# Two more ring buffers, gate exponentials in pieces, six early tiles of the heads' product, and mixed zero products

## The chip, the cores and the metric

The kernel runs on one core of a Trainium2 chip. The metric is device time in microseconds (us), the median of several runs. A profile of one further execution is used for reading; its times are those of that execution.

## The reference

The input is x of 2048 tokens by 512 channels. Two branches are computed and mixed by a gate for each token; everything is float32.

```python
qkv = x @ wqkv                       # 32 heads of 16 channels
p = softmax(q @ k.T * 16 ** -0.5)    # full, 2048 x 2048 for each head
a = (p @ v) @ wo
b = (sigmoid(x @ w_gate) * (x @ w_up)) @ w_down      # 1792 hidden channels
g = sigmoid((x * gate_w).sum(-1))
out = g * a + (1 - g) * b
```

## The kernel before

**Precision.** Products that need float32 accuracy are split: each operand into a high part (type fp32r) and a low part (the remainder), and three products of parts are added up in PSUM. "Split" below means making these two parts, usually a copy on one engine and a subtraction on another (`split`, or `split_later` for steps that are queued for POOL).

**Order.** TensorE, ScalarE (ACT), VectorE (DVE) and GpSimd (POOL) run their instructions in the order in which the program issues them. The DMAs are all issued from SyncE's queue (SP), whose order a scheduler chooses. Tiles come from pools; a tile with a `tag` and `bufs=n` takes the place of the one that was given out n allocations earlier, and its first writer waits until the last user of that one is done, a DMA out of it included.

**The start.** A column `warm` of zeros is set, and `WARM = 10` products of zeros (line 83, 128 x 128 by 128 x 512) go to TensorE while x and the first weights come in. Then queries and keys of the first 128 channels are computed (line 585), then the values `v` and the first maxima.

**The main loop.** It has `NPER = 256` steps k. Heads are taken in pairs, 16 steps for a pair. A step computes eight blocks of scores of 128 x 512 (`st_part`, line 619, four for each head, called t0 and t1 in the orders), whose exponentials ACT writes to `p` (line 621), and at its end the products of p and v (`values`, line 755). The result is copied out of PSUM (`part`, line 760 on ACT; on DVE, line 762, once the maxima have ended) and added up on POOL (line 772). In the same steps TensorE computes scores a second time, ten steps ahead, for the row maxima (`sm_step`, line 268, called m0 and m1), which DVE reduces (line 270). The maxima end ten steps before the last.

**The dense sums.** Beside this a generator `filling` gives out dense products in small sums: queries and keys of the other heads (`qk`), then gate and up products in a scheme with fewer multiplications (`far`, `side`, `chain`), and last `heads`: the product of the attention's result with `wo`, for the first tokens and for the first two of four row blocks. All of these sums use one PSUM bank, `dn`. The matmuls of a sum use half of the PE's rows each (line 152) so that they run beside score matmuls on the other half; d1 are those on the upper half, d0 on the lower. Between the halves `turn` puts a nop on POOL (line 163): it waits for the last matmul of one half, and the first of the other waits for it. So this hand-over stands in POOL's order, behind whatever POOL was given before. `work` hands the queued POOL steps out, after each turn and at the end of each step.

A finished sum is copied out of `dn` by `out_of` (line 429 on DVE, 558 on ACT) into a tile of the ring `er`, which has four buffers, and is then stored to DRAM or added. `put_mix` (lines 332 and 338, tiles `mh` and `ml`) splits mixtures of x during the `far` sums, also into `er`, and stores them to `t_d`.

**The orders.** What TensorE does in a step is written out as a string. `STEADY` has six d1 and six d0 and the maxima; `MORE`, in the three steps after the maxima have ended (k = 246 to 248), has no maxima; `LAST`, in the seven steps after these, has three d1 and three d0. So a sum of twelve half matmuls takes one step in STEADY and MORE and two in LAST. The sums are 252 in all.

**The early hidden chunks.** The hidden layer is processed in 28 chunks. For the first two of them gate and up are loaded at k = 241 (`hidden_load`, into buffers that the queries and keys of a finished pair leave), and `hidden_early` computes the sigmoid in steps: the exponential of the gate on ACT (line 698, 128 x 1024, one call at k = 243 and one at k = 244, issued after the values and their copy), then 16 steps on DVE (lines 702 to 715), one at k = 245 and three in each step from k = 246.

**The tail.** After the loop come 28 chunks of the down projection (line 939), with the hidden layer's sigmoid on ACT (line 691) and its splits, and eight tiles of 256 tokens of the heads' product with `wo` (`heads_out`, line 139). For tiles u < 4, whose first two row blocks were done in the loop and lie in `hp_d`, only the other two are multiplied here, and the stored part is loaded (`had`, one tile of a single buffer) and added (line 922). `finish` applies the gate and stores the output.

Of the kernel before, what the change touches and what calls it, by code (L numbers as in the profile page):

```python
# [25 lines left out]
P = 128  # L26
# [10 lines left out]
WARM = 10  # L37
# [3 lines left out]
BOTH = FREE + 3  # L41
# [5 lines left out]
def gated_mix(ctx, tc, x, xT, wqk, wv, wo, w_gate, w_up, w_down, gate_w, out):  # L47
# [26 lines left out]
    hp_d = dram.tile([8, P, D], F32, name="hp_d")  # L74
# [7 lines left out]
    for _ in range(WARM):  # L82
        pe.matmul(banks[2], z.to_broadcast([P, P]), z.to_broadcast([P, 512]), start=True, stop=True)
# [123 lines left out]
    def put_first(o, dst, c):  # L207

        if c % 2:
            e = [keep.tile([P, 512], F32R, name=f"qe{i}_{c}", tag="er", bufs=4) for i in range(2)]  # L210
        else:
            e = keep.tile([P, 2, 512], F32R, name=f"qe_{c}", tag="ev", bufs=2)
            e = [e[:, i, :] for i in range(2)]
# [115 lines left out]
    def put_mix(n, c, k, t):  # L329
        def high():  # L330
            h = out[n, c, k] = keep.tile([P, 512], F32R, name=f"mh{n}_{c}{k}", tag="er", bufs=4)
# [3 lines left out]
        def low():  # L335
            h = out.pop((n, c, k))
            l = keep.tile([P, 512], F32R, name=f"ml{n}_{c}{k}", tag="er", bufs=4)
# [21 lines left out]
    def filling():  # L359
# [67 lines left out]
        def out_of(run, name):  # L427
            e = keep.tile([P, 512], F32, name=name, tag="er", bufs=4)
# [6 lines left out]
        def sums_of(kind, n, ws):  # L435
# [27 lines left out]
            elif kind == "heads":  # L463
                for u in range(4):
# [49 lines left out]
        def first_heads_split(u):  # L514
            oh, ol, ot, rb = first_heads(u)
            e = keep.tile([P, 2, 256], F32, name=f"of{u}", tag="er", bufs=4)
# [7 lines left out]
        for job, nxt in zip(jobs, jobs[1:]):  # L524
            kind, n = job
            coming = None
            for at, run in enumerate(sums_of(kind, n, ws)):
# [7 lines left out]
                if job == ("chain", pairs[-1]):  # L535
                    if at == 4:
                        for u in range(4):
# [3 lines left out]
                if kind == "heads" and at in (2, 4):  # L541
                    first_heads_split(at // 2 + 1)
# [151 lines left out]
    def hidden_early(m):  # L694
# [3 lines left out]
        act.activation(gate, gate, AF.Exp, scale=-1.0)  # L698
        yield
# [108 lines left out]
    MORE = "t0 d1 t0 d1 d1 t0 d1 d1 t0 d1 turn t1 d0 t1 d0 d0 t1 d0 d0 t1 d0"  # L808
# [6 lines left out]
    for k in range(NPER):  # L815
# [13 lines left out]
        emit(STEADY if k < FREE else MORE if k < BOTH else LAST, **parts)  # L829
# [9 lines left out]
        if k == NPER - 1:  # L839
            break  # L840
        spot[:] = [seven[SUMS]]
        values(k)
        if k == NPER - 15:
            loaded.extend(hidden_load(*chunks[m]) for m in range(2))
            early = [hidden_early(m) for m in range(2)]
        if 192 <= k < 202:
# [5 lines left out]
        if k == NPER - 13:  # L852
            next(early[0])
        if k == NPER - 12:
            next(early[1])
            early = chain(*early)
        if k >= NPER - 11:
# [20 lines left out]
    def heads_load(u):  # L878
        ot = lp.tile([P, KT, 256], F32, name=f"ot{u}", tag="ot")
        rb = lp.tile([P, KT, 256], F32, name=f"rb{u}", tag="rb")  # L880
        ks = slice(2 if u < 4 else 0, KT)
        o_and_r(u, range(KT)[ks], ot[:, ks], rb[:, ks])
        if u < 4:
            had[u] = lp.tile([P, 2, D], F32, name=f"had{u}", tag="had")
            sp.dma_start(had[u], hp_d[2 * u:2 * u + 2].rearrange("a p d -> p a d"))
        return ot[:, ks], rb[:, ks]

    def heads_split(u, ot, rb):
        ks = slice(2 if u < 4 else 0, KT)
# [23 lines left out]
    def heads_out(u, hl):  # L913
        for a in range(2):
            o = bankh()
            cols = slice(a * P, (a + 1) * P)
            ks = range(2 if u < 4 else 0, KT)
# [76 lines left out]
```

## Time and profile before

| | us |
|---|---|
| median of 3 runs | 1703.01 |
| lowest, highest | 1702.22, 1705.33 |
| profiled execution, its own time | 1706.67 |
| span of the profile | 1704.9 |
| ACT, exponentials of scores (line 621), mean of one | 0.63 to 0.65 |
| POOL, additions of values (line 772), mean of one | 1.29 |
| ACT, gate exponentials (line 698), two of them, each | 1.05 |

Times in the profile count from the start of the span. The views used are the page with its engine shares, the waits (who waited for whom), the chain of work that ended last in order of time, the timeline of one engine (start, duration, engine, line, operation, output and inputs, count, and in brackets the idle time before it and what ended it), and the stretches (busy time of each engine between two times, with the clock granted to TensorE and the DMA engines' load). A row of the chain gives the start, the duration, the engine and the line. Half of TensorE's matmuls run beside another one, so a row's duration is not its share of the time; the distance from one start to the next is.

### The profile page before, as it was taken

To read this page: it belongs to the slowest core of one execution; us is meant where nothing else is said; L and a number is where in the kernel's file an instruction comes from. 1 tells how busy PE (TensorE), PEld (TensorE's weight loads), DVE (VectorE), ACT (ScalarE), POOL (GpSimd) and SP (SyncE) were. 2 spreads that over 40 slices of the span, in tenths; PEclk is the share of its full clock that TensorE was granted. 3 is DMA by queue.
4 is the path that set the end of the run, shared out by engine and by line. 5 is a ranking of instruction groups with operands and counts; after the bars stand their busy time and mean duration, and the time that the engine had idled before them with its cause. 6 is when DMAs were issued, how large, how long until landed. Compare 5 with 4: busy or idle time off the path is not lost.

```text
span 1704.9 us, 34507 instructions
## 1 busy us (share of the span) xinstructions
PE 1694.7 (99%) x12498; PEld 1036.1 (61%) x12498; DVE 1446.6 (85%) x2336; ACT 1357.8 (80%) x2638; POOL 883.6 (52%) x865
## 2 busy tenths in 40 slices
PE   9999999999999999999999999999999999999999
PEld 7755555555555555555555555555555555567887
DVE  6988888888789999989888888889988888797643
ACT  4188888888798888988889889889898898884331
POOL 1034343447664555555566666676666666653110
PEclk9999999999999999999999999999999999999999
DMA  9312324254646343433635353535353533458962
GB/s 255 87 40 68 84 63 95 64 126 154 180 151 159 113 106 107 111 116 101 188 104 141 107 143 101 144 107 136 104 126 109 130 113 132 158 186 275 312 199 72
DMA packets 127178, 224.55 MB, mean 132 GB/s; under 512 B 23264, under 2 KB 33248, under 8 KB 124128
## 3 DMA queue, kind: packets, MB, share of 16 engines
q1 hardware_dynamic: 127008, 222.36, 45.4%
q8 instruction: 98, 1.61, 0.4%
q14 instruction: 72, 0.59, 0.1%
HBM read 131.86 MB, written 90.44 MB: 130 GB/s over the span
## 4 chain that ended last, share of the span: by engine, by line
PE 93%; DMA 4%; DVE 2%; SPq 1%; POOL 1%; issue 1%; ACT 0%; DVEq 0%; POOLq 0%; ACTq 0%
PE dn L152 29%; PE sm L755 26%; PE sm L268 12%; PE st L619 7%; PE sm L619 4%; PE sm L939 4%; PE st L268 2%; PE dn L939 2%; PE st L152 1%; PE st L139 1%; DMA gul<-gu_d 1%; PE st L585 1%; PE st L939 1%; PE sm L139 1%; DMA wd0r<-in_w_down_dram 0%
## 5 line engine op out<-in xcount | busy, mean ns | idle before, releaser
L270 DVE TENSOR_REDUCE stat<-sm 128x1 f32<-128x512 f32 x1310 | 848.4, 683 | 161.0 <-PE sm L619 138.7
L621 ACT ACTIVATE p<-st 128x512 f32<-128x512 f32 x1020 | 615.4, 650 | 2.1 <-PE st L619 2.1
L621 ACT ACTIVATE p<-sm 128x512 f32<-128x512 f32 x1026 | 606.4, 626 | 6.1 <-PE st L619 2.8
L268 PE MATMUL sm<-ks,qs 48*128 48x512 f32 x1310 | 522.7, 437 | 0.1
L755 PE MATMUL sm<-p,v 128*17 128x512 f32 x4032 | 483.4, 597 | 0.0
L270 DVE TENSOR_REDUCE stat<-st 128x1 f32<-128x512 f32 x738 | 482.2, 681 | 0.1
L619 PE MATMUL sm<-qs,ks 64*128 64x512 f32 x1026 | 429.5, 421 | 0.7 <-ACT p L621 0.7
L619 PE MATMUL st<-qs,ks 64*128 64x512 f32 x1020 | 427.8, 420 | 0.0
L268 PEld LDWEIGHTS sm<-ks,qs 48*128 48x128 f32 x1310 | 238.5, 184 | 294.1 <-DVE stat L270 208.8
L772 POOL TENSOR_TENSOR sum<-sum,part 128x512 f32<-128x512 f32 x224 | 289.1, 1291 | 184.3 <-PE sm L619 165.6
L268 PE MATMUL st<-ks,qs 48*128 48x512 f32 x738 | 291.6, 395 | 0.0
L760 ACT ACTIVATE part<-sm 128x512 f32<-128x512 f32 x215 | 128.7, 599 | 138.3 <-issue 106.7
L755 PEld LDWEIGHTS sm<-p,v 128*17 128x17 f32 x4032 | 93.5, 97 | 228.1 <-issue 158.7
L619 PEld LDWEIGHTS st<-qs,ks 64*128 64x128 f32 x1020 | 188.0, 184 | 29.4 <-issue 3.4
L619 PEld LDWEIGHTS sm<-qs,ks 64*128 64x128 f32 x1026 | 189.6, 185 | 11.9 <-issue 4.3
L496 POOL TENSOR_TENSOR chain<-chain,chain 128x512 f32<-128x512 f32 x84 | 108.5, 1292 | 114.8 <-PE sm L619 103.7
L268 PEld LDWEIGHTS st<-ks,qs 48*128 48x128 f32 x738 | 137.7, 187 | 1.6 <-ACT p L621 0.4
L496 POOL TENSOR_TENSOR had<-chain,had 128x512 f32<-128x512 f32 x84 | 108.2, 1288 | 55.3 <-PE sm L619 44.3
L496 POOL TENSOR_TENSOR side<-side,side 128x512 f32<-128x512 f32 x28 | 36.2, 1291 | 93.2 <-PE sm L619 89.7
L558 ACT ACTIVATE chain<-dn 128x512 f32<-128x512 f32 x112 | 77.9, 696 | 0.0
L102 POOL TENSOR_TENSOR ol<-ot,oh 128x512 fp32r<-128x512 f32 (+1 forms) x8 | 15.3, 1915 | 99.9 <-ACT oh L99 79.9
L692 DVE TENSOR_TENSOR gul<-gul 128x1024 f32<-128x1024 f32 x26 | 41.7, 1603 | 19.1 <-DMA gul<-gu_d 11.8
(879 smaller groups left out, 3204.9 us busy)
## 6 DMA issues: line engine op xcount, KB each, us to landing
gul<-gu_d SPq DMA_DIRECT2D x56, 512.0 KB
had<-gu_d SPq DMA_DIRECT2D x84, 256.0 KB
gu_d<-had SPq DMA_DIRECT2D x84, 256.0 KB
gu_d<-side SPq DMA_DIRECT2D x56, 256.0 KB
qs<-q_d SPq DMA_DIRECT2D x90, 128.0 KB
ks<-k_d SPq DMA_DIRECT2D x90, 128.0 KB
pv_d<-sum SPq DMA_DIRECT2D x32, 256.0 KB
gu_d<-far SPq DMA_DIRECT2D x28, 256.0 KB
```

Source lines behind the costliest of these rows:

```text
L152: mm = pe.matmul(self.o, a[rows], b[rows], start=(self.n == 0), stop=(self.n == 2 * len(self.ops) - 1))
L268: pe.matmul(t, qs[r:r + KM, qt * P:(qt + 1) * P], ks[r:r + KM, g * 512:(g + 1) * 512], start=True, stop=True)
L270: dve.tensor_reduce(stat[half][:, b, qt % 8, g:g + 1], t, axis=AX.X, op=ALU.max)
L496: pool.tensor_tensor(to, u, w, ALU.add)
L558: leave = lambda e, o: act.activation(e, o, AF.Copy)
L619: pe.matmul(o, ks[r:r + KR, (kt + a) * P:(kt + a + 1) * P], qs[r:r + KR, q0:q0 + 512], start=True, stop=True)
L621: act.activation(pt[:, 2 * a + c, :], o, AF.Exp, scale=DH ** -0.5)
L692: dve.tensor_tensor(gu[:, 1], gu[:, 0], gu[:, 1], ALU.mult)
L755: pe.matmul(o[32 * c:32 * c + VW, :], v[:, 2 * k % 16 + a, h * VW:(h + 1) * VW], pts[c // 2][:, 2 * a + c % 2, :], start=(a == 0), stop=(a ...
L760: act.activation(e, o, AF.Copy)
L772: pool.tensor_tensor(s, s, e, ALU.add)
L939: pe.matmul(down[t], a, b, start=(f == 0 and m == 0), stop=(f == NF - 2 and m == 5))
```

## The change

Four things change.

1. The ring `er` has six buffers, not four, everywhere it is used. In the tail `had` is no tile of its own pool any more: it is two `er` tiles for each u, loaded by two DMAs of 256 KB and not by one of 512 KB.
2. The gate exponentials are issued as four activations of 128 x 256 for each chunk. Two are issued in each of the steps k = 242 to 245, ahead of the values matmuls and so ahead of ACT's copy `part` of that step. The loads move from k = 241 to k = 239. The DVE steps start at k = 243, one a step up to k = 245 and three a step from k = 246.
3. `EARLY = 3`: three tiles of 256 tokens (six sums of 128) are given their first two row blocks in the loop, not four (eight sums). The sums are now 250. `MORE` is gone, and `LAST` is used for all ten steps from k = 246. In the tail u = 3 is multiplied with all four row blocks, and its loads and splits are those of u = 4 to 7.
4. The ten products of zeros are replaced by a mix: twice, four float32 products on the lower 64 rows (one on each strip of 17 columns, 256 wide) and two fp32r products on the upper 64 rows (256 wide); then four of 256 and two of 512 on all rows.

```diff
@@ -34,11 +34,10 @@
 KM = 3 * DH
 KR = 64
 LEAD = 20
-WARM = 10
 NSTEP = NPAIR * 32
 NPER = NSTEP // 2
 FREE = NPER - LEAD // 2
-BOTH = FREE + 3
+EARLY = 3
 HF = NF // 2
 LOW, UP = 0, 1
 
@@ -71,7 +70,7 @@
     k_d = dram.tile([2, D, S], F32, name="k_d")
     gu_d = dram.tile([2, NF, P, S], F32, name="gu_d")
     pv_d = dram.tile([2, NPAIR, P, 512], F32, name="pv_d")
-    hp_d = dram.tile([8, P, D], F32, name="hp_d")
+    hp_d = dram.tile([2 * EARLY, P, D], F32, name="hp_d")
     rec_d = dram.tile([P, 512], F32, name="rec_d")
     t_d = dram.tile([3, 2, 2, 2, P, 512], F32, name="t_d")
     max_d = dram.tile([2 * NPAIR, 4, 32, 2, 32], F32, name="max_d")
@@ -79,8 +78,20 @@
     warm = keep.tile([P, 1], F32, name="warm")
     dve.memset(warm, 0.0)
     z = warm.bitcast(F32R)
-    for _ in range(WARM):
-        pe.matmul(banks[2], z.to_broadcast([P, P]), z.to_broadcast([P, 512]), start=True, stop=True)
+
+    def zeros(o, a, b, r=slice(0, P)):
+        rows, m, n = r.stop - r.start, o.shape[0], o.shape[1]
+        pe.matmul(o, a[r].to_broadcast([rows, m]), b[r].to_broadcast([rows, n]), start=True, stop=True)
+    low, up = slice(0, 64), slice(64, P)
+    for _ in range(2):
+        for c in range(4):
+            zeros(banks[2][32 * c:32 * c + VW, :256], warm, warm, low)
+        for _ in range(2):
+            zeros(banks[1][:, :256], z, z, up)
+    for _ in range(4):
+        zeros(banks[1][:, :256], z, z)
+    for _ in range(2):
+        zeros(banks[2], z, z)
     mpads = [keep.tile([P, 32], F32, name=f"mpad{i}") for i in range(2)]
     mpad = turns(mpads)
     den = keep.tile([P, 512], F32, name="den")
@@ -207,7 +218,7 @@
     def put_first(o, dst, c):
 
         if c % 2:
-            e = [keep.tile([P, 512], F32R, name=f"qe{i}_{c}", tag="er", bufs=4) for i in range(2)]
+            e = [keep.tile([P, 512], F32R, name=f"qe{i}_{c}", tag="er", bufs=6) for i in range(2)]
         else:
             e = keep.tile([P, 2, 512], F32R, name=f"qe_{c}", tag="ev", bufs=2)
             e = [e[:, i, :] for i in range(2)]
@@ -328,13 +339,13 @@
 
     def put_mix(n, c, k, t):
         def high():
-            h = out[n, c, k] = keep.tile([P, 512], F32R, name=f"mh{n}_{c}{k}", tag="er", bufs=4)
+            h = out[n, c, k] = keep.tile([P, 512], F32R, name=f"mh{n}_{c}{k}", tag="er", bufs=6)
             pool.tensor_copy(h, t)
             sp.dma_start(t_d[n, 0, c, k], h.bitcast(F32))
 
         def low():
             h = out.pop((n, c, k))
-            l = keep.tile([P, 512], F32R, name=f"ml{n}_{c}{k}", tag="er", bufs=4)
+            l = keep.tile([P, 512], F32R, name=f"ml{n}_{c}{k}", tag="er", bufs=6)
             pool.tensor_tensor(l, t, h.bitcast(F32), ALU.subtract)
             sp.dma_start(t_d[n, 1, c, k], l.bitcast(F32))
         out = {}
@@ -425,7 +436,7 @@
             return ws[0], ws[2], ws[1], ws[3]
 
         def out_of(run, name):
-            e = keep.tile([P, 512], F32, name=name, tag="er", bufs=4)
+            e = keep.tile([P, 512], F32, name=name, tag="er", bufs=6)
             leave(e, run.o)
             return e
 
@@ -461,7 +472,7 @@
                         else:
                             plus(e, e, first, place(m, i, c + 2))
             elif kind == "heads":
-                for u in range(4):
+                for u in range(EARLY):
                     while split_of[u] in later:
                         later.pop(0)[1]()
                     oh, ol = [t for t in first_heads(u)][:2]
@@ -513,7 +524,7 @@
 
         def first_heads_split(u):
             oh, ol, ot, rb = first_heads(u)
-            e = keep.tile([P, 2, 256], F32, name=f"of{u}", tag="er", bufs=4)
+            e = keep.tile([P, 2, 256], F32, name=f"of{u}", tag="er", bufs=6)
             later.append((1.3, lambda: pool.tensor_tensor(e, ot.bitcast(F32), rb.bitcast(F32), ALU.mult)))
             split_later(oh, ol, e)
             split_of[u] = later[-1]
@@ -534,12 +545,12 @@
                         mix_x(u // 2, u % 2)
                 if job == ("chain", pairs[-1]):
                     if at == 4:
-                        for u in range(4):
+                        for u in range(EARLY):
                             first_heads_load(u)
                     if at in (6, 7):
                         first_heads_split(at - 6)
-                if kind == "heads" and at in (2, 4):
-                    first_heads_split(at // 2 + 1)
+                if kind == "heads" and at == 2:
+                    first_heads_split(2)
                 if at == ask[kind][0]:
                     coming = raws(*nxt)
                 if at == ask[kind][1]:
@@ -695,8 +706,10 @@
 
         gu = loaded[m]
         gate, up = [gu[:, a].rearrange("p f s -> p (f s)") for a in range(2)]
-        act.activation(gate, gate, AF.Exp, scale=-1.0)
-        yield
+        for a in range(4):
+            cols = slice(a * 256, (a + 1) * 256)
+            act.activation(gate[:, cols], gate[:, cols], AF.Exp, scale=-1.0)
+            yield
         two = [slice(a * 512, (a + 1) * 512) for a in range(2)]
         for cols in two:
             dve.tensor_scalar(gate[:, cols], gate[:, cols], 1.0, 3e38, op0=ALU.add, op1=ALU.min)
@@ -805,7 +818,6 @@
     STEADY = ("m1:3 t0:2 m0:4 d1 d1 t0:5 m0:6 d1 d1 t0:1 d1 m0:3 d1 t0:2 turn m0:0 t1:4 "
               "m1:5 d0 d0 t1:1 t1:6 d0 m1:2 d0 m1:3 d0 t1:4 d0")
     SUMS = 0
-    MORE = "t0 d1 t0 d1 d1 t0 d1 d1 t0 d1 turn t1 d0 t1 d0 d0 t1 d0 d0 t1 d0"
     LAST = "t0 d1 t0 d1 t0 d1 turn t0 t1 t1 d0 t1 d0 t1 d0"
 
     parts = {"m0": mx(0), "m1": mx(1), "d0": dense(LOW), "d1": dense(UP)}
@@ -826,7 +838,7 @@
         if n % 32 == 0 and n // 32 + 1 < NPAIR:
             load_pair(n // 32 + 1)
         parts["t0"], parts["t1"] = st_part(k, 0), st_part(k + 1, 1) if k + 1 < NPER else iter(())
-        emit(STEADY if k < FREE else MORE if k < BOTH else LAST, **parts)
+        emit(STEADY if k < FREE else LAST, **parts)
         if run and run.done():
             run = next(fill, None)
         elif run and run.n:
@@ -838,11 +850,15 @@
         soon.clear()
         if k == NPER - 1:
             break
+        if NPER - 15 < k <= NPER - 11:
+            for _ in range(2):
+                next(next(exps))
         spot[:] = [seven[SUMS]]
         values(k)
-        if k == NPER - 15:
+        if k == NPER - 17:
             loaded.extend(hidden_load(*chunks[m]) for m in range(2))
             early = [hidden_early(m) for m in range(2)]
+            exps = iter([early[0]] * 4 + [early[1]] * 4)
         if 192 <= k < 202:
             next(dens[0], None)
         if k == NPER - 6:
@@ -850,11 +866,8 @@
         if k == NPER - 2:
             raws = [late_raw(*late[m][:2]) for m in range(2)]
         if k == NPER - 13:
-            next(early[0])
-        if k == NPER - 12:
-            next(early[1])
             early = chain(*early)
-        if k >= NPER - 11:
+        if k >= NPER - 13:
             for _ in range(1 if k < FREE else 3):
                 next(early, None)
 
@@ -878,15 +891,16 @@
     def heads_load(u):
         ot = lp.tile([P, KT, 256], F32, name=f"ot{u}", tag="ot")
         rb = lp.tile([P, KT, 256], F32, name=f"rb{u}", tag="rb")
-        ks = slice(2 if u < 4 else 0, KT)
+        ks = slice(2 if u < EARLY else 0, KT)
         o_and_r(u, range(KT)[ks], ot[:, ks], rb[:, ks])
-        if u < 4:
-            had[u] = lp.tile([P, 2, D], F32, name=f"had{u}", tag="had")
-            sp.dma_start(had[u], hp_d[2 * u:2 * u + 2].rearrange("a p d -> p a d"))
+        if u < EARLY:
+            had[u] = [keep.tile([P, D], F32, name=f"had{u}_{a}", tag="er", bufs=6) for a in range(2)]
+            for a in range(2):
+                sp.dma_start(had[u][a], hp_d[2 * u + a])
         return ot[:, ks], rb[:, ks]
 
     def heads_split(u, ot, rb):
-        ks = slice(2 if u < 4 else 0, KT)
+        ks = slice(2 if u < EARLY else 0, KT)
         oh = lp.tile([P, KT, 256], F32R, name=f"oh{u}", tag="oh", bufs=2)[:, ks]
         ol = lp.tile([P, KT, 256], F32R, name=f"ol{u}", tag="ol", bufs=2)[:, ks]
         dve.tensor_tensor(ot, ot, rb, ALU.mult)
@@ -914,11 +928,11 @@
         for a in range(2):
             o = bankh()
             cols = slice(a * P, (a + 1) * P)
-            ks = range(2 if u < 4 else 0, KT)
+            ks = range(2 if u < EARLY else 0, KT)
             product(o, [((hl[0][:, n, cols], hl[1][:, n, cols]), (wohl[:, 0, k, :], wohl[:, 1, k, :]))
                         for n, k in enumerate(ks)])
-            if u < 4:
-                h = had[u][:, a]
+            if u < EARLY:
+                h = had[u][a]
                 dve.tensor_tensor(h, o, h, ALU.add)
                 o = h
             finish(2 * u + a, o, g1)
```

## The prediction

> **What bounds the kernel now.** I read the page's engine shares first, then the waits of TensorE, then the chain of work in order of time, then the stretches around each edit. The engine share, from the page:
>
> ```profile
> PE 1694.7 (99%) x12498; PEld 1036.1 (61%) x12498; DVE 1446.6 (85%) x2336; ACT 1357.8 (80%) x2638; POOL 883.6 (52%) x865
> ```
>
> TensorE is never idle to speak of, so an edit pays only where it takes matmuls away, or one of TensorE's few waits, or a stretch in which another engine paces it. The waits of TensorE itself (us in total, times, longest):
>
> ```profile
> PE dn L152 <- POOLq L163: 2.5, 2, 2.1
> PE sm L939 <- DVE hl L102: 1.0, 1, 1.0
> ...
> PE sm L619 <- ACT p L621: 0.7, 2, 0.4
> ```
>
> There are three families: the hand-over nop of a dense sum on POOL (line 163), ScalarE's exponentials, and the tail's splits. What each is worth is read from the chain in order of time. The L755 blocks (16 matmuls of the values) mark the steps k, one block in each:
>
> ```profile
> 381.46 1.84 PE sm L755 x16
> ...
> 395.01 2.16 DMA t_d<-mh
> 399.03 1.84 PE sm L755 x16
> ...
> 443.74 1.89 PE sm L755 x16
> ...
> 454.87 5.71 DMA gu_d<-far
> 464.35 3.54 PE sm L755 x16
> 471.63 1.84 PE sm L755 x16
> 477.21 1.84 PE sm L755 x16
> ...
> 1422.84 1.84 PE sm L755 x16
> ```
>
> An undisturbed step is 477.21 - 471.63 = 5.58 us. From 381.46 to 399.03 are three steps: 17.57, which is 0.83 over 16.74. From 443.74 to 477.21 are five: 33.47, which is 5.57 over 27.90. A DMA out of a buffer of the dense sums' ring stands in the chain both times.
>
> **Part 1, the ring `er` from four to six.** On POOL, ahead of the second stall, and the stretch behind it (columns: us, busy of PE, PEld, DVE, ACT, POOL, then granted clock, DMA share, GB/s):
>
> ```profile
> 455.68 1.27 POOL L338 TENSOR_TENSOR ml<-mix,mh 128x512 fp32r<-128x512 f32 x1
> 460.70 0.61 POOL L332 CAST mh<-mix 128x512 fp32r<-128x512 f32 x1 [3.75 <-DMA gu_d<-far]
> ```
>
> ```profile
> 461.40:464.30 2.90, 2.88 (x15) 1.85 (x16) 1.16 (x2) 1.39 (x3) 2.90 (x3) 0.50 0.50 190
> ```
>
> The cast `mh` takes the slot that a `far` sum left four allocations earlier. That sum's store was issued only at 454.87 and landed 5.71 later. The nop of line 163 stands behind the cast in POOL's order, and TensorE behind the nop. With six slots the cast takes the slot of an allocation two places older, a `far` tile of an earlier step whose store was issued before the jam. The cast would then start at 456.95, when `ml` ends, and the nop would be out at about 457.6; TensorE, which waited 2.1 us until the cast was done at 461.3, came to it at about 459.2. The wait is 2.1 us, yet the excess is 5.57, because the granted clock stands at 0.50 afterwards and a values block takes 3.54 instead of 1.84. [...] The stall at 395.01 is of the same kind (POOL waits for `t_d<-mh`, four allocations back). Both gone: **-6.40**. The bound the other way is 0, if other waits take their place.
>
> **Part 2, the gate exponentials.** Before, two 1024-wide activations stand behind the values copy `part` of steps 243 and 244. After, eight of 256 stand ahead of the copies of steps 242 to 245, two in each. On ScalarE:
>
> ```profile
> 1457.01 0.70 ACT L558 ACTIVATE chain<-dn 128x512 f32<-128x512 f32 x1
> 1458.28 0.60 ACT L760 ACTIVATE part<-sm 128x512 f32<-128x512 f32 x1 [0.58 <-POOL chain L496]
> 1458.78 1.05 ACT L698 ACTIVATE gul<-gul 128x1024 f32<-128x1024 f32 x1
> ```
>
> ```profile
> 1514.22 0.22 ACT L866 ACTIVATE g<-logit 128x16 f32<-128x16 f32 x1
> 1514.34 1.05 ACT L691 ACTIVATE gul<-gul 128x1024 f32<-128x1024 f32 x1
> ```
>
> A 512-wide activation occupies ScalarE for 0.50 us, start to next start (1458.28 to 1458.78), a 16-wide one for 0.12 (1514.22 to 1514.34). In a straight line between them a 256-wide one takes 0.30 and a pair 0.61. The engine is free from 1457.51 (0.50 after the sum's copy began) to 1458.28: 0.77 us, in which `part` waits for the values matmuls. The pair fits. If a piece took all of 0.50, a pair would overrun by 0.23, 0.9 us over four steps. The price of the old place is in the chain rows: from 1422.84 to 1469.31 (next fence) are eight steps, 46.47 against 44.64. That **-1.83** goes; I take no overrun. The old activations were no TensorE stop worth the name (0.4 each), but TensorE was paced by ScalarE until it had caught up.
>
> The gate and up loads move with them, past two steps of SP's queue: four issues of 512 KB, now right behind the early heads' loads, of which a quarter (four) fall away. Queued behind them on SP are loads and stores of `had`, for which POOL's adds and then the line 163 nop wait. VectorE's first three steps of `hidden_early` move into steps 243 to 245, behind the values, where VectorE idles in each step:
>
> ```profile
> 1458.63 0.69 DVE L270 TENSOR_REDUCE stat<-sm 128x1 f32<-128x512 f32 x1 [0.71 <-PE sm L619]
> ```
>
> Two of them are short and lie in that 0.71 us; the third, a reciprocal, comes when the maxima are over. They cost nothing.
>
> **Part 3, six tiles instead of eight, and LAST three steps earlier.** Chain rows, and VectorE's copy of a dense sum:
>
> ```profile
> 1469.31 1.84 PE sm L755 x16
> ...
> 1474.51 1.84 PE sm L755 x16
> ...
> 1484.87 1.84 PE st L755 x16
> ...
> 1488.70 1.84 PE st L755 x16
> ...
> 1492.54 1.84 PE st L755 x16
> ...
> 1496.71 1.84 PE sm L755 x16
> ```
>
> ```profile
> 1493.95 0.68 DVE L429 COPY hp<-dn 128x512 f32<-128x512 f32 x1
> ```
>
> Steps 247 and 248 (MORE) take (1484.87 - 1474.51)/2 = 5.18 each; a LAST step takes 1492.54 - 1488.70 = 3.84. MORE carries a whole dense sum in a step, LAST half of one; with 250 sums, not 252, the remaining four fit into eight LAST steps. Three steps save 3 x 1.34 = 4.02. One LAST step took 4.17: the only bank `dn` was still being copied by VectorE at 1493.95, behind three steps of `hidden_early`. With every sum in LAST steps I add one more such wait: +0.33, net **-3.69**. LAST is eight exponentials a step, so ScalarE paces it.
>
> The missing tiles return in the tail. The heads of u = 3 multiply two row blocks before and four after, as u = 4 already does:
>
> ```profile
> 1605.90 1.36 PE sm L139 x6
> ...
> 1624.94 2.72 PE st L139 x12
> ```
>
> Two tiles of 1.36 become two of 2.72: **+2.72**, all of it on TensorE, which has no gap there. The extra loads, ScalarE and POOL split of u = 3, and the two dropped additions lie beside it. `had` becomes six ring tiles instead of one shared one; that takes waits from SP, or lets those loads run ahead (a rival below).
>
> **Part 4, the mixed zero products.** TensorE, then its weight loads:
>
> ```profile
> 0.92 4.63 PE L83 MATMUL st<-warm 128*128 128x512 f32 x10 [0.92 <-DVE warm L80]
> 5.35 0.63 PE L585 MATMUL st<-xh,q0h 128*128 128x512 f32 x1
> ...
> 7.05 0.50 PE L585 MATMUL st<-xl,q0h 128*128 128x512 f32 x1
> 7.39 0.39 PE L585 MATMUL st<-xh,q0l 128*128 128x512 f32 x1
> ```
>
> ```profile
> 9.24 0.19 PEld L585 LDWEIGHTS st<-xl,q0h 128*128 128x128 f32 x1 [0.29 <-DVE xl L102]
> ```
>
> Ten zeros take (5.35 - 0.92)/10 = 0.44 us each, twice the 0.227 of 2.72/12, up to 7.05. The new ones, at that slow pace: a values block runs two f32 products of 512 columns on each of four strips side by side in 1.84, so one of 256 columns takes 0.46, and 0.92 at half pace; the two fp32r products of half the rows, 0.22 each, run beside it or behind it. Two such rounds are 1.84 to 2.7; then 4 x 0.22 and 2 x 0.44 follow: 3.6 to 4.5 us instead of 4.4. The first product can gain up to 0.35, but at 9.24 the products wait for VectorE's split in any case: **0**.
>
> **Sum.** -6.40 - 1.83 - 3.69 + 2.72 = -9.2 us. The profiled execution took 1706.67 us (span 1704.90, 1.77 around it), so its counterpart comes to 1697.5. It lies 3.66 above the median of 1703.01; I give the unprofiled runs the same difference: **1693.8**.
>
> **The rivals.**
> (a) *The ring's wait is not removed, only moved.* In the same step SP's late issue holds the store, and a sixth slot may be held as well, or POOL's adds may wait for `mix`. For: 3.75 us of POOL waiting is longer than one step's slack. Against: the older slots' stores were issued a step earlier. Then 5.57 stays: 1699.4.
> (b) *The `had` loads run ahead into the tail's opening.*
>
> ```profile
> 1535.00:1560.00 25.00, 23.55 (x103) 18.88 (x103) 17.91 (x15) 8.63 (x9) 8.69 (x3) 1.00 0.95 313
> ```
>
> The DMA engines are 95% busy there at 313 GB/s. Four of the 256 KB loads that now come later would cost 1.05 MB/313 GB/s = 3.3 us: 1697.1. Against: they are issued in the program's order by chunks.
> [...]
> (d) *Slower: ScalarE stands still for the gate load.* The exponentials now precede the copies, so all later exponentials queue behind a late load. The first piece is due at 1457.01 - 5.58 + 0.50 = 1451.9. Chain rows:
>
> ```profile
> 1448.38 0.43 SPq L660
> ...
> 1451.68 7.07 DMA wd0r<-in_w_down_dram
> ...
> 1539.15 9.83 DMA gul<-gu_d
> ```
>
> The load was issued at 1448.38; two steps earlier is 1437.2, and I allow 4 us for the early heads' loads ahead of it: 1441. If SP keeps it back until the place of `wd0r` (1451.68) and it takes the longest 9.83, it lands at 1461.5, 9.6 late, and the half clock adds 5.57 - 2.12 = 3.45: -9.2 + 13.1 = +3.9, 1706.9. It decides from a landing at about 1458 on (9.2 - 3.45 = 5.8 late), where all the gain is gone. Against: 11 us from issue to need.
>
> **How the numbers follow.** About 0.2%, 3.4 us, is what a measurement can tell from no change. Chances: forecast 0.58, (a) 0.14, (b) 0.10, (c) 0.09, (d) 0.09. Faster, below 1699.6: 0.57 + 0.07 + 0.07 + 0.06 = 0.77. Slower, above 1706.4: 0.08 from (d). The rest, 0.15, is the same. Low end: 0.35 at the start, the 1.0 of the tail's wait for `hl` and the 0.33 go too, and 0.8 for the fastest run shown: 1691.3. High end: (a) with 1.1 of the overrun and second copy wait, 1700.5; only (d) and mixtures lie outside.
>
> **What would show it.** Right: no POOL wait for `gu_d<-far` at 460, steps of 5.58 through 455 to 478 with the clock at 1.00; steps 242 to 245 at 5.58 with pieces in the 0.77 us gap; LAST at 3.84 from step 246; tiles of u = 3 at 2.72; first full-pace product near 7. Wrong: a stop over 2 us elsewhere with the clock at 0.50, a piece waiting for `gul<-gu_d`, or the tail's opening with more than the 1.0 us wait for `hl`.

## The result and the profile after

The changed kernel takes 1697.18 us (median of six, 1696.12 to 1698.13). The kernel before took 1706.11 (median of six, 1702.22 to 1708.16); three of these six are the runs shown ahead of the prediction, and the other three took 1706.88 to 1708.16. The medians differ by 8.9 us, where 9.2 was forecast; the ratio is 0.9951 [0.9938, 0.9965], which is 8.4 us with a range of 6.0 to 10.6. The absolute number was 1693.8, and it is 3.4 too low: the three earlier runs had a median of 1703.01, and that of all six lies 3.1 higher. Two further series of the changed kernel gave 1696.83 (0.9957 [0.9943, 0.9970]) and 1697.64 (0.9948 [0.9934, 0.9962]).

The profiled execution of the changed kernel took 1696.12 us (span 1694.3, against 1704.90). Every line of the code now stands 1 to 14 further down: the values are L768 (before L755), the dense sum L163 (L152) and its hand-over nop L174 (L163), the copies `mh` and `ml` L343 and L349 (L332, L338), the gate exponentials L711 (L698), the tail's products L953 (L939) and its first ones L150 (L139). The engine shares from the page, then the waits of TensorE (us in total, times, longest):

```profile
PE 1688.6 (100%) x12502; PEld 1034.9 (61%) x12502; DVE 1446.0 (85%) x2332; ACT 1358.7 (80%) x2644; POOL 881.0 (52%) x862
```

```profile
PE st L84 <- DVE warm L79: 0.9, 1, 0.9
PE dn L630 <- DMA qs<-max_d: 0.3, 1, 0.3
PE dn L953 <- POOL wd5l L113: 0.2, 1, 0.2
PE st L630 <- DVE stat L281: 0.2, 1, 0.2
```

The 2.5 us at the nop, which headed this list before, are gone, and so are the 0.7 for the exponentials and the 1.0 for the tail's split. What is left is smaller than 0.4 except for the start.

**The ring.** The chain of work in order of time, POOL's rows at the place of the old stall (the first is the cast that waited 3.75 us before), and the stretch that followed it (us, busy of PE, PEld, DVE, ACT, POOL, granted clock, DMA share, GB/s):

```profile
454.57 1.84 PE sm L768 x16
...
460.16 1.84 PE sm L768 x16
...
465.74 1.84 PE sm L768 x16
...
471.32 1.84 PE sm L768 x16
```

```profile
456.58 0.61 POOL L343 CAST mh<-mix 128x512 fp32r<-128x512 f32 x1
...
460.74 0.61 POOL L343 CAST mh<-mix 128x512 fp32r<-128x512 f32 x1 [0.93 <-DMA gu_d<-far]
```

```profile
461.40:464.30 2.90, 2.90 (x27) 2.08 (x20) 2.19 (x5) 2.81 (x6) 1.60 (x2) 1.00 0.96 362
```

The steps are 5.58 to 5.59 throughout, the clock is 1.00 where it was 0.50, and TensorE is busy in all of the 2.90 us. The cast starts as soon as POOL has ended `ml`, at 456.58. POOL still waits for the same kind of store twice, 0.93 us for the next cast and 0.66 for the `ml` behind it; in this profile TensorE does not stop for them. The DMA engines are still crowded, 0.96 here, where before they were at 0.89 from 459.00 to 461.40 and at 0.50 behind that: the crowd did not go, it only holds no buffer that is needed at once.

**The exponentials.** ScalarE in one of the four steps, then the chain from there into the LAST steps:

```profile
1451.09 0.70 ACT L569 ACTIVATE chain<-dn 128x512 f32<-128x512 f32 x1
1451.57 0.81 ACT L711 ACTIVATE gul<-gul 128x256 f32<-128x256 f32 x2
1452.36 0.60 ACT L773 ACTIVATE part<-sm 128x512 f32<-128x512 f32 x1
```

```profile
1450.41 1.84 PE sm L768 x16
...
1455.99 1.84 PE sm L768 x16
...
1461.61 1.84 PE sm L768 x16
...
1465.44 1.84 PE sm L768 x16
...
1469.83 1.84 PE sm L768 x16
...
1473.66 1.84 PE st L768 x16
...
1477.49 1.84 PE st L768 x16
```

From the start of the pair at 1451.57 to that of `part` at 1452.36 are 0.79 us, and the gap that the prediction gave it was 0.77. `part` starts with no idle time ahead of it, yet no later than it did: 2.02 us behind the first matmul of its values block in both profiles. The two steps that were 6.49 are 5.58 and 5.62. The LAST pace begins at 1461.61, three steps earlier than before: 3.83, 4.39, 3.83, where the old steps were 5.20, 5.18 and 5.18.

**The tail and the start.** The chain at the heads of u = 3, then TensorE at the very beginning:

```profile
1592.63 2.72 PE sm L150 x12
1595.35 2.72 PE st L150 x12
```

```profile
0.92 5.48 PE L84 MATMUL st<-warm 64*17 64x256 f32 x26 [0.92 <-DVE warm L79]
6.19 0.63 PE L596 MATMUL st<-xh,q0h 128*128 128x512 f32 x1
...
7.90 0.58 PE L596 MATMUL st<-xl,q0h 128*128 128x512 f32 x1
8.31 0.40 PE L596 MATMUL st<-xh,q0l 128*128 128x512 f32 x1
```

The zeros now run until 6.19 and the first real product follows 0.84 later than before; products are at full pace, 0.23 us from one start to the next, from about 8.3, before from about 7.4; until then it is about 0.43 us in both profiles.

Where the time went, by the starts of the values blocks in the two profiles, changed minus before: +0.51 at the first block (the zeros), -5.89 behind both ring stalls (so -6.40 from these), -7.70 when the exponentials are through (-1.81), -11.21 three steps later (-3.51), -11.20 at the last block (1514.08 against 1502.88). From there to the end of the span the tail takes 191.47 us, before 190.82. The two longer tiles are +2.72 of that. Of the other -2.1, some 1.5 are shorter waits of TensorE (0.2 us, before 0.3, 0.5 and 1.0), which the repeats below do not show.

### The profile page after: what moved, and what is told of

Same layout as the page of the kernel before. It is cut to its first block, busy times and chain, and to the rows that moved or that the text cites. A ratio compares the mean times of both kernels' runs of the same rounds, so it can differ in the third digit from the quotient of the medians.

```text
span 1694.3 us, 34493 instructions
## 1 busy us (share of the span) xinstructions
PE 1688.6 (100%) x12502; PEld 1034.9 (61%) x12502; DVE 1446.0 (85%) x2332; ACT 1358.7 (80%) x2644; POOL 881.0 (52%) x862
## 4 chain that ended last, share of the span: by engine, by line
PE 98%; POOL 1%; DVE 0%; issue 0%; DMA 0%; SPq 0%; POOLq 0%; DVEq 0%
PE dn L163 30%; PE sm L768 27%; PE sm L279 12%; PE st L630 7%; PE sm L953 5%; PE sm L630 5%; PE st L279 2%; PE dn L953 2%; PE st L953 2%; PE st L150 1%; PE st L163 1%; PE st L596 1%; PE sm L150 1%; DVE stat L281 0%; PE st L768 0%
## 5 line engine op out<-in xcount | busy, mean ns | idle before, releaser
L768 PE MATMUL sm<-p,v 128*17 128x512 f32 x4032 | 482.1, 595 | 0.0
L768 PEld LDWEIGHTS sm<-p,v 128*17 128x17 f32 x4032 | 93.5, 96 | 227.2 <-issue 157.4
L113 POOL TENSOR_TENSOR ol<-ot,oh 128x1024 fp32r<-128x1024 f32 (+1 forms) x8 | 16.4, 2054 | 102.5 <-ACT oh L110 82.2
L140 POOL CAST qe<-qk 128x512 fp32r<-128x512 f32 x24 | 14.6, 610 | 77.4 <-ACT qk L569 77.4
```

The costliest lines, as they stand in the source:

```text
L768: pe.matmul(o[32 * c:32 * c + VW, :], v[:, 2 * k % 16 + a, h * VW:(h + 1) * VW], pts[c // 2][:, 2 * a + c % 2, :], start=(a == 0), stop=(a ...
```

## The experiments

Each time is the median of its series, and each ratio is to the kernel before, run beside it. "The changed kernel" is abbreviated by its name, changed.

### Four slots again

```
-tag="er", bufs=6
+tag="er", bufs=4
```

The edit stands at all six places where the ring is allocated.

> The changed kernel with the ring back at four buffers; all else stays. Theory (the ring's depth made the two stalls): POOL waits again for the store of a far tile and for that of a mixture tile, the two stalls return with +0.8 and +5.6 us in steps 53 to 68, the clock stands at 0.50 after the second, and the time is 1697.2 + 6.4 = 1703.6, ratio to the kernel before about 0.999. Rival (the stalls came from a jam of the transfers that one profile happened to show): steps 53 to 68 stay at 5.58, ratio about 0.995.

Measured: 1701.62 us, 0.9980 [0.9971, 0.9990]. The stalls are back in their old places. TensorE's waits, POOL's row, and the stretch behind:

```profile
PE dn L163 <- POOLq L174: 2.6, 2, 2.2
```

```profile
461.21 0.61 POOL L343 CAST mh<-mix 128x512 fp32r<-128x512 f32 x1 [3.79 <-DMA gu_d<-far]
```

```profile
459.50:462.00 2.50, 0.30 (x4) 0.07 (x2) 1.84 (x4) 0.85 (x2) 0.71 (x2) 1.00 0.93 345
462.00:464.20 2.20, 2.20 (x15) 1.33 (x19) 1.18 (x2) 1.41 (x3) 2.20 (x2) 0.66 0.41 155
464.20:468.00 3.80, 3.80 (x26) 1.33 (x27) 0.62 (x2) 1.66 (x4) 2.05 (x3) 0.75 0.41 143
```

TensorE is busy in 0.30 of 2.50 us while POOL's cast waits for the store, and then works at 0.66 to 0.75 of its clock. The first stalled step takes 6.42, the second and the one behind it 8.88 and 6.53: 0.84 and 4.25 over the undisturbed 5.58. A step among the exponentials takes 6.74, 1.16 over, which neither profile had. At the last values block this kernel is 6.14 us behind changed. So the ring is the cause of the two old stalls. They cost 5.09 in this execution and 6.40 in the profile of before, where the clock fell lower, and the second costs about twice its own idle time. The median over all ten executions is 4.4 us above that of changed, where 6.4 was expected: both profiles show executions that are slower than the median of their kernel (1703.75 against 1701.62, and 1706.67 against 1706.11).

### Five slots, and `had` in a buffer of its own

```
-tag="er", bufs=6
+tag="er", bufs=5
...
-            had[u] = [keep.tile([P, D], F32, name=f"had{u}_{a}", tag="er", bufs=6) for a in range(2)]
-            for a in range(2):
-                sp.dma_start(had[u][a], hp_d[2 * u + a])
+            had_u = lp.tile([P, 2, D], F32, name=f"had{u}", tag="had")
+            had[u] = [had_u[:, a] for a in range(2)]
+            sp.dma_start(had_u, hp_d[2 * u:2 * u + 2].rearrange("a p d -> p a d"))
```

> The changed kernel with the stored parts of the early tiles (had) in one buffer of their own again, loaded by one transfer of 512 KB, and the ring at five buffers, since six do not fit beside it. Theory (in the changed kernel these loads went out before the loop ended, which relieved the crowded opening of the tail): the waits of TensorE at the tail's opening return, +1.0 to 1.7 us between the last values block and the end, ratio about 0.996. Rival (the tail's waits went because VectorE was earlier there): the tail keeps its length, ratio 0.995. With five buffers the stalls of steps 53 to 68 stay away if one more buffer is enough; the place of any stall tells the two apart.

Measured: 1703.41 us, 0.9986 [0.9977, 0.9995]. Five slots remove the first stall (5.58) but not the second (7.28). The waits, and the stretch behind the second stall:

```profile
PE sm L953 <- DVE hl L113: 2.1, 2, 1.1
PE dn L163 <- POOLq L174: 1.3, 1, 1.3
```

```profile
459.85:462.50 2.65, 2.65 (x23) 1.45 (x27) 1.63 (x3) 1.86 (x4) 2.65 (x3) 1.00 0.63 241
```

The idle time is 1.26 us here and the clock stays at 1.00, so that this stall costs only 1.7. That is one execution: five of this kernel's ten show a mean clock of 0.998 or 0.999, and those five took 1703.64 to 1704.46 us, where the other five took 1699.09 to 1703.17. A step with the exponentials took 6.20, and the tail is 196.1 us long, the longest of all runs, with 2.1 us of waits for VectorE's split. The two edits were not separated, so the longer tail may be the shared `had` buffer or chance; this run settles the ring alone.

### The pieces behind the values' copies

```
+        spot[:] = [seven[SUMS]]
+        values(k)
         if NPER - 15 < k <= NPER - 11:
...
-        spot[:] = [seven[SUMS]]
-        values(k)
```

> The changed kernel with its eight 256-wide exponentials issued behind the values copy, two in each of the same four steps. Theory (it is the place that counts, since ScalarE is idle only ahead of the copy): each pair holds up the score exponentials by about 0.6 us, steps 243 to 246 take 0.4 to 0.6 longer each, +1.6 to 2.4 us in all, ratio about 0.9963. Rival (the smaller pieces are what helps): these steps stay at 5.58, ratio 0.995.

Measured: 1700.49 us, 0.9969 [0.9959, 0.9980]. ScalarE:

```profile
1453.05 0.60 ACT L773 ACTIVATE part<-sm 128x512 f32<-128x512 f32 x1 [0.56 <-POOL xl L137]
1453.54 0.71 ACT L711 ACTIVATE gul<-gul 128x256 f32<-128x256 f32 x2
```

The gap of 0.56 stands empty ahead of `part`, the pair lies behind it, and three steps take 6.16 instead of 5.6. At the last block this kernel is 2.1 us behind changed, 1.7 more than at the first one: the gain comes from the place, not from the smaller pieces.

### Ten plain zeros

```
-    for _ in range(2):
-        for c in range(4):
-            zeros(banks[2][32 * c:32 * c + VW, :256], warm, warm, low)
-        for _ in range(2):
-            zeros(banks[1][:, :256], z, z, up)
-    for _ in range(4):
-        zeros(banks[1][:, :256], z, z)
-    for _ in range(2):
+    for _ in range(10):
         zeros(banks[2], z, z)
```

> The changed kernel with the ten plain products of zeros of before. Theory (the mix holds TensorE longer, and that is a small loss): the first real product starts at 5.35 as before, not at 6.19, the first values block about 0.5 us earlier than the changed kernel's 91.36, time 0.5 us less, ratio about 0.9948. Rival (the mix opens the clock sooner or gains elsewhere): first values block at 91.4 or later, time the same or up to 1 us more.

Measured: 1698.30 us, 0.9958 [0.9943, 0.9973]. The first values block is at 90.56, 0.80 before changed (0.5 was expected), but the whole is not faster: its step of 4.39 takes 5.51, and the tail's opening has 2.3 us of waits. The chain shows what the long step waits for (lines of this kernel stand 8 further up):

```profile
1462.11 0.23 DVE mpad L277
...
1463.28 2.54 DMA max_d<-mhl
...
1465.83 0.70 SPq L295
...
1466.59 1.94 DMA qs<-max_d
...
1468.66 0.47 PE sm L622
```

The last half's maxima go through DRAM to the other partitions, 6.55 us from VectorE's `mpad` to the product that reads them. In the LAST pace that no longer fits a step.

### Without the loads of the last maxima

The last half's maxima are written but not read back; its scores use what lies in the buffer.

```
-            for b in (1, 0):
+            for b in (1, 0) if half != (NPAIR - 1, 1) else ():
```

> The changed kernel without the loads that carry the last row maxima (of the last pair's second half) from DRAM into the queries' rows: the last pair's second half then takes the maxima of an earlier pair. Theory (step 247 is long because TensorE waits for this trip, which three MORE steps covered before): step 247 falls from between 4.4 and 5.5 to 3.84. Rival (the wait is for the hand-over on POOL or for VectorE's copy of dn, as the prediction had it): step 247 stays at 4.3 or more.

Measured: 1699.55 us, 0.9969 [0.9953, 0.9985]. The step still takes 4.26, where the theory had 3.84; in the three profiles of changed it takes 4.39, 4.49 and 4.42. POOL and the weight loads of this kernel, then the same two rows of changed and a later weight load of its step:

```profile
1467.54 0.61 POOL L140 CAST xh<-of 128x512 fp32r<-128x512 f32 x1
```

```profile
1468.26 0.18 PEld L163 LDWEIGHTS dn<-wo1h,xh 64*128 64x128 f32 x1 [0.27 <-POOLq L174]
```

```profile
1466.91 0.61 POOL L140 CAST xh<-of 128x512 fp32r<-128x512 f32 x1
```

```profile
1467.63 0.18 PEld L163 LDWEIGHTS dn<-wo1h,xh 64*128 64x128 f32 x1 [0.24 <-POOLq L174]
...
1468.64 0.18 PEld L630 LDWEIGHTS sm<-qs,ks 64*128 64x128 f32 x1 [0.48 <-ACT p L632]
```

In both, the nop is released when POOL ends the cast that begins the split of the heads u = 2. In changed the first of the scores t1 then waits 0.48 us. The profile names the exponentials, but the loads of the last maxima let go of it at nearly the same time, and the run without these loads has no such wait there. So two things hold the step: the hand-over through POOL, which keeps it at 4.26 when the trip is gone, and the trip, which adds 0.13 to 0.23 in these profiles. (A step among the exponentials took 6.19 here, which goes against the gain of the trip; what made it longer was not traced.)

### Eight early tiles and the three MORE steps again

```
-EARLY = 3
+EARLY = 4
+BOTH = FREE + 3
...
-        emit(STEADY if k < FREE else LAST, **parts)
+        emit(STEADY if k < FREE else MORE if k < BOTH else LAST, **parts)
```

> The changed kernel with eight early sums of 128 tokens (EARLY = 4) and three MORE steps again, all else as changed. Theory (the prediction's third part): steps 246 to 248 take 5.18 again, about 3.5 us more in the loop, and the tail is 2.7 us shorter, +0.8 in all, ratio about 0.9956. Rival (the part is worth nothing or a loss, since the tail's matmuls come back in full): ratio at or below 0.9951.

Measured: 1701.71 us, 0.9982 [0.9973, 0.9991], 4.9 us above the series of changed in the same session (1696.83). I had expected 0.8. The three steps came back as 5.18 to 5.19 and the tail was shorter, but two steps among the exponentials took 6.53 and 7.17. A new wait, on POOL (lines one further down):

```profile
1450.15 1.29 POOL L508 TENSOR_TENSOR had<-chain,had 128x512 f32<-128x512 f32 x1 [5.10 <-DMA had<-gu_d]
```

The load of `had` is queued on SP behind sixteen head loads and four gate loads of 512 KB, and the DMA engines are 100% busy from 1440 to 1448. POOL stands 5.10 us, and the nop and TensorE behind it. In changed the same row has 2.31, which its slack absorbs.

### The same with the four head loads of u = 3 left out

As above, but the early tiles of u = 3 are computed from what lies in their buffers.

```
-                        for u in range(EARLY):
+                        for u in range(EARLY - 1):
                             first_heads_load(u)
```

> The run with eight early sums and MORE, but without the four loads of the fourth tile's heads in the loop (that tile is computed from whatever lies there). Theory (four more loads of the heads ahead of the gate loads make the load of had late, POOL waits for it, and TensorE for POOL's nop): steps 243 and 244 fall from 6.53 and 7.17 back to 5.58, and the time is 2 to 3 us below the run with sixteen loads, ratio about 0.9967. Rival (the eighth and seventh sum's own work on POOL makes these steps long): they stay at 6.5 and 7.2.

Measured: 1698.22 us, 0.9955 [0.9942, 0.9969]. The same row:

```profile
1445.35 1.29 POOL L508 TENSOR_TENSOR had<-chain,had 128x512 f32<-128x512 f32 x1 [1.12 <-DMA had<-gu_d]
```

The two steps are 5.58 and 5.65 again, with the three MORE steps still in place. So the four head loads that part 3 drops are what makes room for the gate loads that part 2 brings forward. With all sixteen, the two steps were 6.53 + 7.17 - 11.16 = 2.54 over, more than the 1.83 that the old place of the exponentials cost. The whole is 0.6 us above changed in the same session (1697.64): with those four loads gone, part 3 is worth about the 0.8 that I had expected of it, which is too little to tell from nothing.

### Two attempts at a better version

Eight plain zeros, eight early tiles and MORE in two steps:

```
-EARLY = 3
+EARLY = 4
+BOTH = FREE + 2
...
+    for _ in range(8):
         zeros(banks[2], z, z)
...
-        emit(STEADY if k < FREE else LAST, **parts)
+        emit(STEADY if k < FREE else MORE if k < BOTH else LAST, **parts)
```

> A version meant to beat both: the changed kernel with eight plain products of zeros, EARLY = 4, and MORE in steps 246 and 247 only, so that the last maxima's trip lies under longer steps and the tail is spared 2.7 us. Theory: first values block 0.8 to 1.2 us earlier than the changed kernel, steps 246 and 247 at 5.18 each instead of 3.83 and 4.4 to 5.5 (+0.9 to 2.1), tail 2.7 shorter: 1.4 to 3 us less than the changed kernel in the same job, ratio about 0.9938. Rival (VectorE or the hand-overs hold the last sums, which now end in the last step): the gain is lost at the loop's end.

Measured: 1702.09 us, 0.9982 [0.9974, 0.9991]. Two long steps among the exponentials, as with all sixteen head loads (6.15 and 7.00), and a step of 9.18 at the end of the loop, in which TensorE waits 2.25 us for VectorE's copy of a dense sum. Its clock there, and just behind:

```profile
1504.00:1506.60 2.60, 0.35 (x3) 0.04 (x1) 2.56 (x4) 2.57 (x6) 0.88 (x1) 1.00 0.60 202
1506.60:1510.00 3.40, 3.40 (x20) 2.30 (x24) 3.27 (x4) 3.40 (x6) 1.78 (x2) 1.00 0.68 204
```

Eight plain zeros, and the split of u = 2 queued one sum earlier:

```
-                if kind == "heads" and at == 2:
+                if kind == "heads" and at == 1:
                     first_heads_split(2)
```

> A second version meant to beat both: the changed kernel with eight plain products of zeros and the third tile's split queued one dense sum earlier. Theory (step 247 waits for the nop behind that split on POOL): first values block at 90.6 instead of 90.8 to 91.4, step 247 at 3.9 instead of 4.4, 0.7 to 1.5 us less than the changed kernel in the same job, ratio about 0.9945. Rival: the last maxima's trip through DRAM shows in step 247 instead, which stays at 4.3 to 5.5, and nothing is won.

Measured: 1698.29 us, 0.9956 [0.9943, 0.9968]. The hand-over now holds the step before, which took 4.41, and in the next one TensorE waited 1.5 us: this step took 5.69. The profile puts that wait down to ScalarE's exponentials. The loads of the maxima were issued at 1466.84, 1.0 later than in changed, and the last of them let go of TensorE within 0.1 us of the exponentials, so which of the two held it is not shown. Nothing is won, as the rival had it. The second wait stands right behind the first.

### The changed kernel again, twice

Without an edit, in the sessions of the later experiments:

> The changed kernel once more, as the base for the other runs of this job and for how much the opening of the tail differs between executions of one program. If the early loads of had cured the tail's opening, no wait over 0.5 us stands there again; if its first profile was a lucky one, waits for hl of 1 us or more are back, as in the other runs with the same tail. Ratio 0.995.

> The changed kernel once more, as the base of this job. Ratio 0.995; first values block near 91, step 247 near 4.4, waits at the tail's opening between 0 and 2.3 us.

Measured: 1696.83 and 1697.64 us. The long LAST step is there both times (4.49, 4.42), so it belongs to the kernel. The waits at the opening of the tail are 0.51 + 0.71 and 0.34 + 0.65 + 1.05 us, against 0.23 in the first profile: that one was lucky by 1 to 2 us, and with 192.8 and 193.8 us these tails are 2.0 and 3.0 longer than that of before, which fits the +2.72. In the third profile POOL's cast at the place of the old stall waits 1.52 us for the store, not 0.93, and the step there takes 5.97. The first weight load of the dense sum in that step waits for ScalarE's copy of the sum before, so this is not shown to come from POOL, but the room that six slots leave is small.

## Why the prediction was right, and where not

**The ring: right.** Mechanism and place are as worked out: undoing it alone brought the stalls back. The size between the two profiles is the forecast one (-6.40), which it had to be, since the price was read from the same profile of before. By medians the ring is worth about 4.4. The term is thus that of an execution in which the clock fell far, and that the whole came out at 8.9 for 9.2 is in part luck. Rival (a) is out: POOL's waits that stay (0.93 and 0.66) did not stop TensorE in the first profile. The price of the falling clock was read from the rows of before, and the experiments show as well that the idle time alone does not give it: 2.2 us of idle (four slots) cost 4.25 in two steps at 0.66 to 0.75 of the clock, 1.26 us of idle (five slots) cost 1.7 at 1.00.

**The exponentials: right in size (-1.81 for -1.83), but short of a condition.** The pair fits its gap: `part` comes no later than before. Rival (d) did not come: the loads were issued at 1434.10, 7 us before what I allowed, and no piece waited. The prediction named `had` behind those loads on SP, and POOL and the nop behind `had`, and put no price on it. With sixteen head loads that price is the 2.54 us of the two steps. Part 3 paid it in advance, and the prediction summed the parts as if they stood alone.

**LAST three steps earlier: right in size (-3.51 for -3.69), the extra wait for another reason.** I added 0.33 for the copy of the bank `dn`; 0.56 came, at a different step. It is the nop behind POOL's split of u = 2, and for a smaller part the trip of the last maxima. MORE's 5.18 us steps had covered both: the cover that a removed stage gave was not on my list. This is the mis-sized term, small here.

**The tail: +2.72 right** on the tiles. The sum took no change of the waits at its opening. They vary by up to 2 us between executions of one kernel, and the lucky first profile made the span shrink by 10.6. Rival (b) had the loads of `had` run ahead into that opening. They do run ahead, but further. SP's rows:

```profile
1487.40 0.42 SPq L899 DMA_DIRECT2D had<-hp_d  x1
...
1495.28 0.99 SPq L899 DMA_DIRECT2D had<-hp_d  x2
```

They go out while the loop's last steps run, not in the crowded opening; before, the first of them was issued at 1543.44. Whether that helps stays open: the one run that undid it (five slots) had the longest tail, but changed two things.

**The zeros: mis-sized.** I gave them 3.6 to 4.5 us, the upper end with the products on the upper rows behind those on the lower ones; they took 5.27. They did run one after the other, and each kind took longer than I had it: 0.72 for two products on the upper rows (0.44 in the sum), 0.98 for the four strips (0.92), 1.01 for the four of 256 columns (0.88). Of the chances, the 0.09 of (c) and its 0.07 in the sum for a faster kernel stand for a loss by a long start at half pace. No run shows such a loss: in the first profile full pace comes 0.9 us later (8.3 for 7.4), and the first block 0.51. Where it comes is not fixed either: with the same ten plain zeros it is 7.4 in the profile of before, and in that of the run with ten plain zeros the first product, at 5.27, has it already (0.25 us to the next). The first block lies at 90.83 to 91.92 in the nine profiles with the mix and at 90.56 to 90.85 in the four with plain zeros, so the mix costs some tenths of a us. On the whole time nothing shows: plain zeros gave 1698.30.

**The absolute time: 3.4 too low** because I took a difference that was read from a slow execution of before (1706.67) and carried it over to a median of three faster ones. The prediction's own counterpart of the profiled execution, 1697.5, is 0.3 from the measured median. That the 1697.1 of rival (b) is as near is chance: from 1524 to 1549 of the first profile the DMA engines are as busy as before (0.95 at 313 GB/s), and TensorE is busy in all of the 25 us. In the series beside the first four experiments the kernel before took 1706.4 on average where the mean granted clock of the execution was 0.998 (10 runs), 1705.0 at 0.999 (9) and 1702.7 at 1.000 (3). By an estimate from these numbers, a mean of 0.998 over 1705 us is 3.4 us of clock (0.002 x 1705). So the clock does not fall equally in every execution; why is not shown. That the three runs shown held more of the lucky kind is likely, but their clocks are not on record. Changed stood at 1.000 in 16 of 17 executions.

## What to carry to other kernels

Count a ring's depth in allocations from the oldest store that may be late, and price a stall by the idle time and by the clock behind it: four and five slots failed here, six were enough, with little to spare. A price read from one profile is that of one execution: compare its time with the median first. When a stage is shortened, list what its length covered on every queue (here a DRAM trip, a split on POOL, a copy), for the next one stands right behind. Before moving large loads earlier, ask what is queued behind them and which edit makes the room: two parts that look independent may pay for each other.

## What the runs showed of the hardware

Idle gaps of 2.1 and 2.2 us in TensorE were followed by a granted clock of 0.50 (before) and 0.66 to 0.75 (four slots); a gap of 1.26 us was not (1.00), and one of 2.25 us elsewhere was not either (1.00 from 1506.60 to 1510.00). These are single executions. Over all executions of the three kernels whose profile shows a gap over 2 us, the mean granted clock stayed below 1.000 in 49 of 57 (before), 9 of 10 (four slots) and 9 of 11 (the kernel of the 2.25 us). With five slots it was 5 of 10, in changed 1 of 17, in five other kernels, whose longest wait was 1.5 us or less, 1 of 31 together, and without the loads of the last maxima 0 of 4. So in these kernels a mean clock below 1.000 was more frequent where the profile has a gap over 2 us, but not in every execution, and what decides a single one is not settled here.

f32 products on rows 0 to 63 and fp32r products on rows 64 to 127, into different banks, did not overlap when they were zeros at the start of changed: the four strips started at 0.92, the two on the upper rows at 1.90, the second round at 2.62 and 3.60, and what follows at 4.32. A round took 0.98 + 0.72 = 1.70 us, while products of 512 columns went at 0.43 us each (0.23 from 8.3 on).

From the issue of the last store of 32 KB of maxima to that of the loads behind it 1.45 us passed in changed (1464.38 to 1465.83) and 3.36 before (1471.47 to 1474.83). With ten plain zeros the store took 2.54 us; there the trip through DRAM from one partition to the others took 5.4 us from the store's issue to the product (1463.28 to 1468.66), and 6.55 from VectorE's first step (1462.11).
